# Linear attention and a top-1 mixture of experts on one core: loads in one queue, routing in small steps, scatters and fetches of separate rows told apart

## The chip, the cores and the metric

The kernel runs on 1 core of one Trainium2 chip. The metric is the device time of one execution in microseconds (us), as a median of several runs. The engines are TensorE (PE), VectorE (DVE), ScalarE (ACT), GpSimd (POOL) and SyncE (SP), which issues DMAs. Each has its own in-order list of instructions.

## The reference

Decayed linear attention over B = 4, H = 8, S = 768, D = 64, then every token goes through one of 8 experts.

```python
for b in range(nb):                       # blocks of the sequence
    intra = (qb @ kb.T * Dmask) @ vb
    out[:, :, sl] = intra + (qb * lam_pow) @ kv_state
    kv_state = lam_block * kv_state + (kb * rev_pow).T @ vb
x = out as (B*S = 3072 tokens) x (H*D = 512)
logits = x @ w_gate + modality_bias[modality_id]
e_idx = argmax(logits); gate_w = softmax(logits)[e_idx]
for e in range(8):                        # F = 1024
    out[mask] = gate_w[mask, None] * (relu(x[mask] @ w1[e]) @ w2[e])
```

With the seed's inputs four experts get tokens: 1,494, 1,319, 253 and 6.

## The kernel before

**Attention.** The kernel takes the sequence in chunks of 128: 24 blocks `g`, loaded in 12 pairs `m` by `load(m)`, 2 MB each, into `SLOTS` = 4 rotating buffers with the tag "load". Pairs 0 to 2 come in halves, pair 3 whole, on SP's queue; later pairs on ACT's. For a block, `scores` (PE, tile s), `mask` (DVE, pt), `keys` (ACT, kd), `query` (POOL, qd), `products` (PE, kv), `add` (DVE, state), `from_state` and `values` (PE, tile o; ACT copies to xt). After two pairs `turns` transposes their output on PE (`turn`, and line 303 and 305 copies to grp) and does the gate products (`gates`, tile x).

**Routing.** Tokens are routed in three batches of eight row tiles. `choose` finds each token's expert (one-hot `oh`), `ranks` counts on PE the tokens ahead of each in its expert, `slots_of` makes row numbers. `one_slot` then scatters one row tile, 128 rows of 528 floats, from grp to `placed` in DRAM by an indirect DMA on POOL; `jobs` is the list of scatters to do, `go`, `need` and `tick` take from it. `count` (PE) sums the tokens of each expert so far. After batch 0 `early_list` finds two tiles that are full (list A: tiles 0 and 1), after batch 1 two more (list B: tiles 2 and 3), after batch 2 `late_list` the rest (list C): tiles 4 and 5 of 64 and 32 rows (the thins), eight wide tiles 6 to 13, and up to nine more behind a branch. `put` puts a routing operation of DVE in a queue and `do(n)` gives out the next n of it.

**Experts.** A wide tile is 256 rows. `fetch_x` fetches its rows (xg, and idx for token and gate), `fetch_w1` and `fetch_w2` the expert's weights (raw1, raw2; the DMAs of a tile whose expert is that of the one before are skipped by a condition). `turn_rows` transposes the rows on DVE, `split_rows` and `split_w1` make two halves of each operand (ACT rounds, DVE subtracts). `first_layer` does four quarters on PE, `second` each 128 rows with three products per operand pair, then ACT scales by the gate (y) and POOL stores by token. Tile 0's first layer is done whole, without halves. `thin_first` and `thin_second` do the thins, their weights for tile 5 in `both1` and `both2`. `clear_ends` writes empty rows behind the last row of each expert, 8 DMAs of 256 rows with a register load each.

**What sets the order.** PE, DVE, ACT and SP execute in the order in which the code is written (`manual_schedule`); POOL's order is held by `pool`. DMAs wait for data by dependencies that the framework finds; two groups tell it that their rows differ (`apart`). In `placed`, every scatter and every fetch is otherwise a reader or writer of the same tensor, so a fetch stands behind all scatters written before it.

## Time and profile before

| | us |
|---|---|
| median of 3 runs (436.13 to 437.58) | 436.2 |
| the profiled execution | 436.5 |
| its span | 434.8 |
| TensorE busy | 398.2 |
| VectorE busy | 267.1 |
| ScalarE busy | 210.5 |
| GpSimd busy | 98.7 |

The span is from the first to the last recorded event; 1.7 us of the execution lie around it. Busy time counts an engine's own work and not its waits; matmuls overlap their weight loads. A stage's row gives the busy time of every engine inside it, and `PEclk` the share of the full TensorE clock that was granted. Stages of before, in us from the span's start: start to 33.5, pairs 2 to 11 to 115.9, tile 0 to 142.7, tile 1 to 172.3, tile 2 to 194.9, tile 3 to 219.8, thins to 244.8, wide tiles 6 to 13 to 424.6, end at 434.8.

### The profile page before, as it was taken

Reading aid. Unit: us, or ns where it says so; the run is one execution under the profiler, and the core shown is the slowest. Engines: PE = TensorE matmul, PEld = TensorE weight load, DVE = VectorE, ACT = ScalarE, POOL = GpSimd, SP = SyncE. Lnnn points to the kernel's source line nnn. Section 1 sums busy time; section 2 is a strip of 40 time slices with the busy share of each in tenths; the row PEclk is TensorE's granted clock in tenths of the full one; section 3 lists DMA queues with packets and bytes.
Section 4 is the critical chain, followed back from the end, with each engine's and each line's share of the span. In section 5 each row is a group of like instructions: output and inputs, shape, how many; then the busy total and the mean of one; then the engine's idle time right before and its main releaser. Section 6 shows DMA issues by size and latency. Waiting matters only on the chain.

```text
span 434.8 us, 9729 instructions
## 1 busy us (share of the span) xinstructions
PE 398.2 (92%) x3597; PEld 347.6 (80%) x3597; DVE 267.1 (61%) x494; ACT 210.5 (48%) x411; POOL 98.7 (23%) x125
## 2 busy tenths in 40 slices
PE   6879989699799979998968999999999999999990
PEld 4779879588588968978833798989898989898980
DVE  5638759777477656888320676667666666767510
ACT  1529568485445426418220646464646465555510
POOL 2815215550440238302000102020202020101000
PEclk8989999899899969999995999999999999999996
DMA  7998776947358973457359008787302020200100
GB/s 257 388 404 298 272 272 261 389 172 277 122 172 275 338 283 150 124 200 260 76 171 295 11 11 261 214 248 224 98 14 74 26 73 26 73 26 3 48 27 20
DMA packets 38216, 75.38 MB, mean 173 GB/s; under 512 B 6926, under 2 KB 19726, under 8 KB 37904
## 3 DMA queue, kind: packets, MB, share of 16 engines
q1 hardware_dynamic: 29728, 40.92, 29.7%
q10 hardware_dynamic: 4512, 20.97, 12.8%
q0 software_dynamic: 3920, 12.78, 7.7%
q8 instruction: 30, 0.49, 0.5%
q14 instruction: 26, 0.21, 0.2%
HBM read 90.57 MB, written 17.84 MB: 249 GB/s over the span
## 4 chain that ended last, share of the span: by engine, by line
issue 48%; PE 19%; DVE 11%; DMA 8%; POOL 6%; ACT 4%; POOLq 1%; ACTq 0%; SPq 0%; DVEq 0%
POOL out_dram L713 6%; DMA load<-in_qkv_dram 5%; DMA raw<-in_w_dram 3%; PE o L281 3%; PE o L299 2%; PE s L239 2%; PE s L689 2%; ACT kd L229 2%; PE o L273 2%; PE kv L689 2%; DVE pt L243 2%; DVE state L261 1%; DVE grp L303 1%; ACT xt L285 1%; DVE w2l L581 1%
## 5 line engine op out<-in xcount | busy, mean ns | idle before, releaser
L581 DVE TENSOR_TENSOR w2l<-raw,w2h 128x1024 fp32r<-128x1024 f32 x48 | 58.7, 1223 | 35.5 <-ACT w2h L580 34.8
L713 POOL DMA_INDIRECT out_dram<-y,idx x24 | 31.0, 1290 | 214.1 <-ACT y L712 191.1
L669 PE MATMUL o<-w2h,hh 128*128 128x512 f32 x192 | 75.2, 391 | 0.0
L670 PE MATMUL o<-w2l,hh 128*128 128x512 f32 x192 | 75.1, 391 | 0.0
L671 PE MATMUL o<-w2h,hl 128*128 128x512 f32 x192 | 74.9, 390 | 0.0
L581 DVE TENSOR_TENSOR w1l<-raw,w1h 128x1024 fp32r<-128x1024 f32 x44 | 51.3, 1222 | 3.6 <-ACT w1h L580 3.5
L669 PE MATMUL kv<-xh,w1h 128*128 128x256 f32 x176 | 51.1, 290 | 0.0
L669 PE MATMUL s<-xh,w1h 128*128 128x256 f32 x176 | 49.9, 284 | 1.1 <-ACT w1h L580 1.1
L670 PE MATMUL kv<-xl,w1h 128*128 128x256 f32 x176 | 50.7, 288 | 0.0
L671 PE MATMUL kv<-xh,w1l 128*128 128x256 f32 x176 | 50.5, 287 | 0.0
L671 PE MATMUL s<-xh,w1l 128*128 128x256 f32 x176 | 49.7, 282 | 0.8 <-DVE w1l L581 0.8
L580 ACT CAST w2h<-raw 128x1024 fp32r<-128x1024 f32 x48 | 49.8, 1038 | 0.0
L670 PE MATMUL s<-xl,w1h 128*128 128x256 f32 x176 | 49.7, 282 | 0.0
L580 ACT CAST w1h<-raw 128x1024 fp32r<-128x1024 f32 x44 | 43.1, 1045 | 1.7 <-DMA raw<-in_w_dram 1.7
L671 PEld LDWEIGHTS o<-w2h,hl 128*128 128x128 f32 x192 | 36.2, 188 | 7.6
L669 PEld LDWEIGHTS o<-w2h,hh 128*128 128x128 f32 x192 | 36.2, 189 | 7.3
L670 PEld LDWEIGHTS o<-w2l,hh 128*128 128x128 f32 x192 | 36.2, 188 | 7.2
L669 PEld LDWEIGHTS kv<-xh,w1h 128*128 128x128 f32 x176 | 34.1, 194 | 4.0 <-issue 3.8
L712 ACT ACTIVATE y<-o,idx 128x512 f32<-128x512 f32 x24 | 16.3, 683 | 42.1 <-PE o L671 42.1
L229 ACT ACTIVATE kd<-load,dk 128x64 f32<-128x64 f32 x144 | 35.6, 336 | 0.8 <-ACT grp L305 0.6
L216 POOL TENSOR_TENSOR qd<-load,pq 128x512 f32<-128x512 f32 x20 | 25.5, 1275 | 42.2 <-PE o L273 22.4
L669 PEld LDWEIGHTS s<-xh,w1h 128*128 128x128 f32 x176 | 33.0, 187 | 2.1 <-ACT w1h L580 1.6
(220 smaller groups left out, 674.2 us busy)
## 6 DMA issues: line engine op xcount, KB each, us to landing
raw<-in_w_dram SPq DMA_DIRECT2D x96, 512.0 KB
load<-in_qkv_dram ACTq DMA_DIRECT2D x8, 2048.0 KB
xg<-placed SPq DMA_DIRECT2D x48, 128.0 KB
placed<-blank SPq DMA_DIRECT2D x9, 528.0 KB
load<-in_qkv_dram SPq DMA_DIRECT2D x8, 512.0 KB
raw<-in_w_dram ACTq DMA_DIRECT2D x2, 2048.0 KB
both<-in_w_dram SPq DMA_DIRECT2D x8, 512.0 KB
load<-in_qkv_dram SPq DMA_DIRECT2D x2, 1024.0 KB
```

What stands on the lines that cost most here:

```text
L216: pool(nc.gpsimd.tensor_tensor(out=qds[g], in0=loaded(g)[1], in1=pq, op=ALU.mult))
L229: nc.scalar.activation(out=kds[g][:, p, hl, :], in_=kn[:, p, hl, :], func=AF.Copy, scale=dk[:, hl, p, P - 1 : P])
L239: nc.tensor.matmul(scs[g][:, hl, p, :], kt[r, p, :], qt[r, p, :], start=True, stop=True)
L281: nc.tensor.matmul(op[place(g, hl), p, :], vt[:, (2 * p + hl) * D : (2 * p + hl + 1) * D], pt[:, hl, p, :], start=(c == 0 and p == 0), sto ...
L580: nc.scalar.copy(out=hi, in_=src)
L581: nc.vector.tensor_tensor(out=lo, in0=src, in1=hi.bitcast(F32), op=ALU.subtract)
L669: nc.tensor.matmul(out, ah, bh, start=first, stop=False)
L670: nc.tensor.matmul(out, ah, bl, start=False, stop=False)
L671: return nc.tensor.matmul(out, al, bh, start=False, stop=last)
L689: mm = nc.tensor.matmul(hp[:, j, :], raw1[:, i, kc, fs], xt2[:, kc, :], start=(kc == 0), stop=(kc == KC - 1))
L712: nc.scalar.activation(out=y, in_=yp, func=AF.Copy, scale=idx[:, t, 1:2].bitcast(F32))
L713: sc = nc.gpsimd.indirect_dma_start(out=out, out_offset=bass.IndirectOffsetOnAxis(ap=idx[:, t, 0:1], axis=0), in_=y, in_offset=None, bound ...
```

## The change

1. All loads of q, k, v and of tile 0's weights go to SP's queue, the latter in four pieces of 512 KB and not one of 2,048 KB. `lamh` goes to ACT's.
2. The start is written out in another order; five more dummy matmuls; the identity is made first on POOL; a block's `query` waits for its first score product.
3. The routing's DVE work is given out in steps (`do(7)` per pair, `do(5)` after turns, `do(4)` in tiles), with fewer operations (`running` is a scan in place of a product and a sum). Ranks, counts and lists stand at other pairs, and so do the scatters (`aside`).
4. Scatters of batch b and fetches for lists A and B get groups of their own, so that a fetch waits for the scatters of its own batch and earlier ones alone. `xg` has two buffers. `fetch_x(0)` is at pair 8, `fetch_x(1)` at pair 9, `turn_rows(0)` at pair 10.
5. The last `turns` and its gates move inside tile 0's first layer; `ranks` of batch 2 come behind that layer, `count` behind the first quarter of tile 1.
6. Each clear becomes two, 64 rows always and 192 rows under a condition, each with a register load. `both1` is fetched ahead of `raw2` of tile 4, `both2` right behind it, into buffers of their own.
7. The last store of the fixed tiles goes to its own buffer and is issued behind the branches.
8. The scratch for POOL's DMA descriptors (`dynamic_dma_scratch_size`) is set to 2048; before, it is not given.

The core of the diff, with pieces left out that only rename, and the pieces that shorten the lists:

```diff
-                (nc.sync if m < SLOTS else nc.scalar).dma_start(out=halves[m], in_=source(m))
+                nc.sync.dma_start(out=halves[m], in_=source(m))
...
+                op = pool(nc.gpsimd.tensor_tensor(out=qds[g], in0=loaded(g)[1], in1=pq, op=ALU.mult))
+                if g in begun:
+                    after(op, begun.pop(g))
...
-            apart("slots", sc)
+            b = c // RC
+            for group in [f"slots{i}" for i in range(b + 1)] + [f"list{i}" for i in range(b)]:
+                tc.declare_no_dep(sc.ins, group=group, reason="rows differ")
+            tc.add_to_no_dep_group(f"slots{b}", sc.ins)
             return pool(sc, free=True)
...
-        def clear_ends():
-
-            for e in range(E):
-                vr = nc.sync.value_load(ends_at[0:1, e : e + 1], min_val=0, max_val=E * CAP - TT)
-                apart("ends", clear(bass.ds(vr, TT)))
+            if n < EARLY:
+                for f in fetches:
+                    for b in range(n // SOON + 1, RN):
+                        tc.declare_no_dep(f.ins, group=f"slots{b}", reason="rows differ")
+                    tc.add_to_no_dep_group(f"list{n // SOON}", f.ins)
+
...
+        def clear(at, rows, **kw):
+
+            p = rows // max(1, (rows + P - 1) // P)
+            return nc.sync.dma_start(out=placed[at, :].rearrange("(r p) w -> p r w", p=p),
+                                     in_=blank[:p].unsqueeze(1).to_broadcast([p, rows // p, RW]), **kw)
+
+        def clear_end(e):
+            vr = nc.sync.value_load(ends_at[0:1, 0, e : e + 1], min_val=0, max_val=E * CAP - TT)
+            for i in range(2):
+                if i == 0:
+                    c = clear(bass.ds(vr, XT), XT)
+                else:
+                    cr = nc.sync.value_load(ends_at[0:1, 1, e : e + 1], min_val=0, max_val=1)
+                    c = clear(bass.ds(vr + XT, TT - XT), TT - XT, cond=cr)
+                apart("ends", c)
+                for b in range(RN):
+                    tc.declare_no_dep(c.ins, group=f"slots{b}", reason="rows differ")
+                for b in range(2):
+                    tc.declare_no_dep(c.ins, group=f"list{b}", reason="rows differ")
...
                     tick(mm)
-            y = work.tile([P, DM], F32, name="y", tag="qd", bufs=4)
+            if hold:
+                y = const.tile([P, DM], F32, name="held")
+            else:
+                y = work.tile([P, DM], F32, name="y", tag="qd", bufs=4)
             nc.scalar.activation(out=y, in_=yp, func=AF.Copy, scale=idx[:, t, 1:2].bitcast(F32))
-            sc = nc.gpsimd.indirect_dma_start(
-                out=out, out_offset=bass.IndirectOffsetOnAxis(ap=idx[:, t, 0:1], axis=0),
-                in_=y, in_offset=None, bounds_check=N - 1, oob_is_err=False)
-            apart("tokens", sc)
-            pool(sc, free=True)
+
+            def store():
+                sc = nc.gpsimd.indirect_dma_start(
+                    out=out, out_offset=bass.IndirectOffsetOnAxis(ap=idx[:, t, 0:1], axis=0),
+                    in_=y, in_offset=None, bounds_check=N - 1, oob_is_err=False)
+                apart("tokens", sc)
+                pool(sc, free=True)
+
+            if hold:
+                behind.append(store)
+            else:
+                store()
         def thin_first(x, w):
```

```diff
         keys(0, True)
         scores(0)
         mask(0)
+        keep_busy(5)
         powers()
         from_state((0,))
         values(0)
+        block(1, True)
         products(0)
-        scores(1)
-        query(1)
-        keys(1, True)
         add(0)
-        mask(1)
+        scores(2)
+        mask(2)
+        query(2)
         from_state((1,))
         values(1)
         products(1)
-        for m in range(pairs):
+        keys(2)
+        add(1)
+        block(3)
+        gpsimd_constants()
+        load(SLOTS)
+        products(2)
+        products(3)
+        add(2)
+        add(3)
+        from_state((2, 3))
+        values(2)
+        values(3)
+        turns(0)
+        block(4)
+        block(5)
+        load(1 + SLOTS)
+        products(4)
+        products(5)
+        add(4)
+        for m in range(2, pairs):
             a, b = HB * m, HB * m + 1
             ahead = m + 1 < pairs
             add(b)
             if m == 4:
                 routed = 0, *choose(0, gate_rows())
-            elif m == 6:
+            elif m == 8:
+                routed = 1, *choose(1, gate_rows())
+            if ahead:
+                block(a + 2)
+                block(b + 2)
+            if m == 2:
+                routing_constants()
+            elif m == 3:
+                clear(slice(E * CAP, E * CAP + TT), TT)
+            elif m == 5 or m == 9:
+                ranks(routed[-1])
                 slots += slots_of(*routed)
                 jobs += [("slots", one_slot)] * RC
-            elif m == 7:
+            elif m == 6:
+                count()
                 early = early_list("A", listA)
-            elif m == 8:
-                routed = 1, *choose(1, gate_rows())
             elif m == 10:
-                slots += slots_of(*routed)
-                jobs += [("slots", one_slot)] * RC
-            if m == 0:
-                keys(2)
-                keys(3)
-            if ahead:
-                for i, g in enumerate((a + 2, b + 2)):
-                    scores(g)
-                    mask(g)
-                    if m > 0:
-                        keys(g)
-                    query(g)
-            do()
+                count()
+                early = early_list("B", listB, early)
+            do(7)
             go(aside.get(m, (0, 0))[0])
-            if m == 0:
-                gpsimd_constants()
-            else:
-                if m == 2:
-                    routing_constants()
-                from_state((a, b))
-                for g in (a, b):
-                    values(g)
-            if m == 3:
-                clear(slice(E * CAP, E * CAP + TT))
-            elif m == 5 or m == 9:
...
                 add(a + 2)
             go(aside.get(m, (0, 0))[1])
-            if m % 2:
+            if m % 2 and ahead:
                 turns(m // 2)
-            if m == 6:
-                count()
-            elif m == 8:
+                do(5)
+            if m == 8:
                 raw1 = w1_part("raw1", F32)
-                fetch_w1(*fetch_regs(0, True, nc.scalar), eng=nc.scalar)
+                fetch_w1(*fetch_regs(0, True))
+                fetch_x(0)
             elif m == 9:
                 raw2 = w2_part("raw2", F32)
-                fetch_w2(*fetch_regs(0, True, nc.scalar), eng=nc.scalar)
```

```diff
         def amid0(i):
-            nonlocal routed, slots, early
+            nonlocal routed, slots
+            if i < 2:
+                for tb in (2 * i, 2 * i + 1):
+                    turn(GR - 1, tb)
+                if i == 0:
+                    gates(GR - 1)
+                do(6)
+            elif i == 2:
+                do()
+                routed = 2, *choose(2, gate_rows())
+                do(4)
+            else:
+                do()
+
+        def amid1(i):
             if i == 0:
-                count()
-                early = early_list("B", listB, early)
-                do(10)
-            else:
-                do(8)
-
-        def amid1(i):
-            nonlocal routed, slots
-            if i == 0:
-                routed = 2, *choose(2, gate_rows())
-            elif i == 1:
-                do()
-            elif i == 2:
-                ranks(routed[-1])
-                slots += slots_of(*routed)
                 do()
                 jobs.extend([("slots", one_slot)] * RC)
                 count()
+                late_list(*early)
+            else:
+                do(4)
         def amid2(i):
-            if i == 0:
-                late_list(*early)
-            if i < 3:
-                do(12)
-            else:
-                do()
+            do(4)
         first_layer(amid0, whole=True)
+        need("slots")
         fetch_w1(*fetch_regs(1))
         fetch_w2(*fetch_regs(1))
+        fetch_x(2)
+        ranks(routed[-1])
         turn_rows(1)
         split_rows()
-        split_w1()
+        slots += slots_of(*routed)
+        split_w1(1)
+        fetch_w1(*fetch_regs(2))
         for t in range(2):
             second(0, t)
-        do()
-        fetch_x(2)
-        fetch_w1(*fetch_regs(2))
         first_layer(amid1)
         fetch_w2(*fetch_regs(2))
+        fetch_x(3)
         turn_rows(2)
         split_rows()
-        split_w1()
+        split_w1(4)
+        fetch_w1(*fetch_regs(3))
         for t in range(2):
             second(1, t)
```

```diff
         first_layer(amid2)
         fetch_w2(*fetch_regs(3))
         turn_rows(3)
         split_rows()
-        split_w1()
-        clear_ends()
-        for n in range(thins, wides + 1):
-            fetch_x(n)
+        split_w1(4)
+        for e in range(E):
+            clear_end(e)
         fetch_w1(*fetch_regs(thins))
         for t in range(2):
             second(2, t)
-
+        do()
+
+        both1 = w1_part("both1", F32, True)
+        both2 = [work.tile([P, 2, 2, DM], F32, name="both2", tag="xt", bufs=2) for i in range(2)]
+        both2 = [both2[i // 2][:, i % 2] for i in range(4)]
         first_layer()
+        for n in range(thins, wides + 1):
+            fetch_x(n)
+        fetch_w1(*fetch_regs(thins + 1, True), to=both1)
         fetch_w2(*fetch_regs(thins))
-        both1 = w1_part("both1", F32, True)
-        fetch_w1(*fetch_regs(thins + 1, True), to=both1)
+        fetch_w2(*fetch_regs(thins + 1, True), to=both2)
...
                 if n + 2 < fixed_ones:
                     fetch_w1(*fetch_regs(n + 2))
...
+        for store in behind:
+            store()
...
-    nc = _bacc.Bacc("TRN2", target_bir_lowering=False, num_devices=1)
+    nc = _bacc.Bacc("TRN2", target_bir_lowering=False, num_devices=1, dynamic_dma_scratch_size=2048)
```

Three places show how instructions move. In the rows, s and kv are the first layer's products, x the small tile of the routing, o the second layer's, hh and hl the two halves of the hidden layer, raw the weights as fetched.

PE, the end of tile 0's first layer. Before, with the count for list B behind its first quarter:

```order
L689 MATMUL s<-xt_127,raw_1387 128x256 x8
L422 LDWEIGHTS onesb
L422 MATMUL x<-ohsum,onesb 128x8
L689 MATMUL kv<-xt_127,raw_1387 128x256 x8
L689 MATMUL s<-xt_127,raw_1387 128x256 x8
L689 MATMUL kv<-xt_127,raw_1387 128x256 x8
L669 MATMUL o<-w2h,hh_1807 128x512
```

and after, with the last turn and the ranks of batch 2:

```order
L713 MATMUL s<-xt_127,raw_1390 128x256 x8
L312 MATMUL o<-ident,xt 128x128 x8
L323 MATMUL x<-xt,wgq 32x128 x16
L713 MATMUL kv<-xt_127,raw_1390 128x256 x8
L312 MATMUL o<-ident,xt 128x128 x8
L713 MATMUL s<-xt_127,raw_1390 128x256 x8
L713 MATMUL kv<-xt_127,raw_1390 128x256 x8
L375 LDWEIGHTS lowb
L375 MATMUL x<-oh,lowb 128x64
L376 LDWEIGHTS onesb
L376 MATMUL x<-ohsum,onesb 128x64
```

The count left the layer; between its last products and the second layer stand now the ranks, which read `oh`.

DVE, tile 1's first layer and the routing of batch 2. Before:

```order
L581 TENSOR_TENSOR w2l<-raw_1556,w2h 128x1024
L697 SCALAR_TENSOR_TENSOR hl_1810<-s,hh_1808 128x512
L335 TENSOR_TENSOR pos<-oh,x 128x64
L335 TENSOR_REDUCE slot<-pos 128x8
L335 TENSOR_SCALAR m8s<-m_2093 128x8
L335 TENSOR_REDUCE ohn<-oh 128x8
L335 TENSOR_TENSOR ohsum<-ohsum,ohn 128x8
L335 TENSOR_REDUCE sm<-l 128x8
```

and after:

```order
L597 TENSOR_TENSOR w1l<-raw_1390,w1h 128x1024
L348 TENSOR_REDUCE ohn<-oh 128x8
L597 TENSOR_TENSOR w2l<-raw_1590,w2h 128x1024
L721 SCALAR_TENSOR_TENSOR hl_1795<-s,hh_1793 128x512
L348 TENSOR_TENSOR ohsum<-ohsum,ohn 128x8
L348 TENSOR_REDUCE sm<-l 128x8
```

`ohsum`, which the count on PE reads, stands behind the third quarter's `hl` before, and behind the first quarter's after.

SP, the clears of tile 2's time. Before, two of the eight:

```order
L615 TENSOR_LOAD ends_at
L615 ISA x2
L609 ISA
L609 DMA placed<-blank 256x1x528
L615 TENSOR_LOAD ends_at
L615 ISA x2
L609 ISA
L609 DMA placed<-blank 256x1x528
```

and after, one expert's:

```order
L637 TENSOR_LOAD ends_at
L637 ISA x2
L633 ISA
L633 DMA placed<-blank 64x528
L642 TENSOR_LOAD ends_at
L642 ISA x2
L633 ISA
L633 DMA placed<-blank 96x2x528
```

Behind them, before, the last issues ahead of tile 5's first weights:

```order
L652 DMA raw_1556<-in_w_dram 128x1024
L652 ISA
L652 DMA raw_1556<-in_w_dram 128x1024
L652 ISA
L652 DMA raw_1556<-in_w_dram 128x1024
L632 TENSOR_LOAD listC
L632 ISA x2
L644 ISA
L644 DMA both_2969<-in_w_dram 128x1024
```

and after, the last of those weights and what follows:

```order
L672 DMA both_2854<-in_w_dram 128x1024
L672 ISA
L672 DMA both_2854<-in_w_dram 128x1024
L664 TENSOR_LOAD listC
L664 ISA x2
L667 TENSOR_LOAD listC
L667 ISA x2
L676 ISA
L676 DMA raw_1590<-in_w_dram 128x1024
```

One clear became two loads and two DMAs, and `raw` of the second layer no longer stands ahead of `both`.

## Rows read from the trace of the kernel before

**Rows 1.** The page, part 1: TensorE's busy time, its share of the span, instructions.

```profile
PE 398.2 (92%) x3597; PEld 347.6 (80%) x3597; DVE 267.1 (61%) x494; ACT 210.5 (48%) x411; POOL 98.7 (23%) x125
```

**Rows 2.** Stages: length, busy us (x instructions) by engine, PE's clock, DMA share, GB/s.

```profile
0.00:33.47 33.47, 26.59 (x347) 21.25 (x347) 17.36 (x43) 10.91 (x34) 13.74 (x37) 0.90 0.95 351
33.47:115.93 82.46, 74.39 (x1379) 65.52 (x1379) 62.23 (x152) 54.79 (x187) 30.76 (x36) 0.98 0.71 261
115.93:142.72 26.79, 26.79 (x115) 22.64 (x116) 18.37 (x43) 11.51 (x15) 7.83 (x13) 0.94 0.65 225
142.72:172.27 29.55, 25.88 (x156) 23.63 (x156) 17.61 (x33) 12.50 (x17) 12.99 (x15) 0.88 0.74 250
...
194.90:219.76 24.86, 22.96 (x146) 20.57 (x148) 15.26 (x20) 11.82 (x16) 4.04 (x3) 1.00 0.48 159
219.76:244.84 25.08, 19.14 (x167) 9.63 (x167) 3.71 (x6) 5.43 (x9) 1.97 (x2) 0.73 0.64 203
244.84:424.63 179.79, 179.79 (x1156) 164.17 (x1152) 114.36 (x123) 95.03 (x124) 21.61 (x16) 1.00 0.29 88
```

**Rows 3.** The same view for stretches in which the granted clock was half.

```profile
25.30:28.60 3.30, 3.30 (x43) 2.97 (x39) 0.77 (x1) 0.28 (x1) 0.00 (x0) 0.50 1.03 408
83.30:86.60 3.30, 3.30 (x26) 2.97 (x27) 1.97 (x4) 2.23 (x8) 0.15 (x1) 0.50 1.03 422
117.40:120.70 3.30, 3.30 (x9) 2.64 (x8) 0.32 (x1) 0.00 (x0) 2.75 (x5) 0.50 0.44 169
...
226.60:240.20 13.60, 11.48 (x54) 4.71 (x56) 0.69 (x1) 0.38 (x1) 0.00 (x0) 0.50 0.87 282
```

**Rows 4.** Timeline of PE: start, us, operation, times; in brackets idle before, releaser.

```profile
23.64 0.60 PE L239 MATMUL s<-load 64*128 64x128 f32 x6 [2.86 <-DMA load<-in_qkv_dram]
...
82.53 1.70 PE L299 MATMUL o<-ident,xt 128*128 128x128 f32 x8 [3.57 <-ACT grp L305]
...
115.93 4.98 PE L689 MATMUL s<-xt,raw 128*128 128x256 f32 x14 [1.99 <-DVE xt L657]
...
155.41 0.17 PE L422 MATMUL x<-ohsum,onesb 128*128 128x8 bf16 x1 [3.66 <-DVE ohsum L335]
...
231.09 3.19 PE L729 MATMUL s<-both,xf 128*32 128x256 f32 x25 [0.70 <-DMA both<-in_w_dram]
```

**Rows 5.** Timeline of SP's queue (issues), tiles 2 and 3.

```profile
188.01 11.66 SPq L609 DMA_DIRECT2D placed<-blank  x8
202.43 1.93 SPq L598 DMA_DIRECT2D xq<-placed  x4
...
216.81 1.36 SPq L644 DMA_DIRECT2D raw<-in_w_dram  x4
...
222.09 1.98 SPq L644 DMA_DIRECT2D both<-in_w_dram  x4
```

**Rows 6.** Batch 0's scatters: landing (line 394), two issues, SP's fetch behind them.

```profile
DMA to landing us min/median/max: 4.5/7.2/9.1
...
73.91 0.98 POOL L394 DMA_INDIRECT placed<-grp,sloti  x1 [0.28 <-ACT kd L229]
...
75.39 1.07 POOL L394 DMA_INDIRECT placed<-grp,sloti  x1 [0.28 <-POOL grp L393]
...
100.81 2.49 SPq L598 DMA_DIRECT2D xg<-placed  x4
```

**Rows 7.** Timeline of ACT and DVE: a quarter's end, two routing operations.

```profile
131.85 0.60 ACT L696 ACTIVATE hh<-kv 128x512 fp32r<-128x512 f32 x1 [1.92 <-PE kv L689]
132.48 0.69 DVE L697 SCALAR_TENSOR_TENSOR hl<-kv,hh 128x512 fp32r<-128x512 f32 x1 [0.66 <-ACT hh L696]
...
151.09 0.22 DVE L335 TENSOR_TENSOR oh<-eq,m 128x64 bf16<-128x64 f32 x1
...
155.19 0.17 DVE L335 TENSOR_TENSOR ohsum<-ohsum,ohn 128x8 bf16<-128x8 bf16 x1
```

**Rows 8.** Timeline of POOL: the last store.

```profile
425.63 0.99 POOL L713 DMA_INDIRECT out_dram<-y,idx  x1 [4.45 <-ACT y L712]
```

187 lines of the change are left out of this document (96 added, 91 removed).

## The prediction

> **What bounds the kernel now.** I read the header of the page first: TensorE (PE) is busy for 398.2 us of the span [rows 1]. So time can come only from PE's idle time (36.6 us), from stretches in which its clock was granted at half, and from the two ends. The table by stage says where [rows 2]. The eight wide tiles at the end are PE from end to end at a granted clock of 1.00: 179.79 us, 22.47 us each. That is the price of a tile, and every early tile above it has slack: tile 1 takes 29.55, tile 3 24.86. The pairs m = 2 to 11 hold 82.46 - 74.39 = 8.07 us of PE idle, the start 6.88, the thin section 5.94. A second table gives the clock [rows 3]: stretches of 3.3 us at 0.50 (1.2 of 2.4 GHz) lie at 25.3, 83.3 and 117.4, and 13.6 us around the thins. Each follows a wait of PE. A half-clock stretch of 3.3 us costs up to 1.65 us.
>
> The waits themselves are in PE's timeline [rows 4]: 2.86 us for a load in the start; 3.57 before the turn of pair 7, where VectorE (DVE) was busy with list A; 1.99 before tile 0, for the transpose of its tokens; 3.66 before the count in tile 1, for `ohsum`; and the last of the waits for `both1` in the thins. Then I read SP's queue over tiles 2 and 3 [rows 5], which decides when `both1` comes, the scatters [rows 6], two short DVE and ACT chains [rows 7], and the tail [rows 8].
>
> **The change, part by part.** All against the profiled execution, 436.5 us (span 434.8 and 1.7 around it); that is 0.3 over the median of 436.2.
>
> *Start.* Blocks 2 to 5 are put in another order, so that the state and value products of blocks 2 and 3 and turn 0 stand ahead of the scores that waited 2.86 us for their load [rows 4]. More work than the wait is moved ahead of it, so the wait goes, and the half clock behind it (1.65) with it [rows 3]: **-4.5**. Bounds: -2, if the loads, already 351 GB/s in this stage [rows 2], come no sooner and a part of the wait comes back at pair 3; -6, if the extra five dummy products also save some of the 1 to 2 us waits around block 0.
>
> *Pairs.* The routing of a batch is done in small steps between the pairs' own DVE work, with fewer operations. The 3.57 us went on DVE doing list A in one go; it goes. The 1.99 us before tile 0 go, since the tokens are fetched during pair 8 and turned during pair 10. Of the remaining 2.5 us I leave 1.0. That is -7.1, and -1.65 for the half clock at 83.3: **-8.7**. What hides the moved work: DVE is busy 62.23 of the 82.46 us [rows 2], so it has some 20 us to spare; if the steps fall in front of a block's mask, the cover is gone and waits of that size stay (bound -4). Turn 5 and its gate products move into tile 0: PE's work, the same on either side, nothing.
>
> The cover of the early fetch is thinner. In before the fetch for tile 0 was issued at 100.81, when the last scatter of batch 0 had landed [rows 6]. After, all eight are issued by pair 8, by my count at about 79; with the longest landing of 9.1 us [rows 6] that is 88, and with some 5 us for the fetch and 1.3 for the turn about 95, before tile 0's start at about 99. Three to four us to spare. SP's queue waits in that fetch meanwhile, and the four pieces of `raw2` stand behind it; they are wanted only some us after tile 0's start.
>
> *Tile 0.* Its half clock at 117.4 followed the 1.99 us wait: -1.65. New: PE does the ranks of batch 2 right behind the first layer and must wait there for the one-hot `oh`, which DVE makes after the last quarter's `hl`. From the rows: about 0.2, the ACT pass `hh` 0.60, `hl` 0.69, two steps of 0.22 [rows 7], about 1.9. Bounds: 0, if DVE does the two steps ahead of `hl`; 3.66, the wait that the same thing cost in tile 1 of before [rows 4]. I take +1.9, the chain as the order has it. Together **+0.25**.
>
> *Tile 1.* It falls to a plain tile's 22.47 from 29.55, -7.1 [rows 2]: the 3.66 us wait goes with the half clock behind it, and the weights are asked for earlier. The count still stands on PE, after the first quarter, behind `hh` 0.60, `hl` 0.69 and `ohsum` 0.17 [rows 7] with about 0.2 of passing on: +1.65. **-5.4**.
>
> *Tiles 2, 3 and the thins* go by SP's queue, not by PE. In before the clears start at 188.01 and `both1` is first issued at 222.09 [rows 5], 34.1 us later: eight clears with their register loads 11.7, loads of the lists 2.8, three fetches 14.4 (with the two loads ahead of `raw`), `raw1` skipped 1.4, then `raw2` skipped and three more loads, 3.9. After, each clear is two DMAs and two register loads. A skipped issue is 0.34 (four in 1.36), a register load 0.6 to 0.85 (the 3.9 us less four skipped issues, by three, with or without their set-up): a skipped clear 0.95 to 1.2, and I take 1.0. A clear that is done takes 1.46, one of 64 rows somewhat less, 1.25. By the seed's counts two of the eight second clears are done: 8 x 1.25 + 6 x 1.0 + 2 x 1.46 = 18.9, of which 0.8 is the first load, ahead of the first issue. Then `raw1` with its loads 2.9, the three fetches 13.6, `both1` 1.05, `raw2` now behind it: 35.7, which is +1.6 (bounds -2 and +6, for clears of 15 and 23.4). On the other side the chain starts sooner: DVE does 4 list operations per quarter in tile 2 and not 12, which I put at -2.3 (8 x 0.2 to 0.3, the size of `oh` [rows 7]). So from tile 2's start to tile 6's start, 72.6 us in before [rows 2]: **-0.7** (bounds -5 and +4). Tile 3's own 2.4 us over a plain tile [rows 2] are gained by PE and given back in the wait for `both1`, since tile 3 then ends 44.9 us after tile 2's start and `both1` is issued at about 49.
>
> *Wide tiles:* 0. *Tail.* PE ends at 424.63 [rows 2], 10.2 us before the end of the span. In before the last store is issued until 426.62 [rows 8], and 8.2 us follow: its landing, and the branches over the conditional tiles and the close. After, the branches come first. Nothing shows how the 8.2 divide; bounds 0 and -5. The landing no longer stands ahead of the branches, so I take **-3.0**. *New clock loss:* one stretch of half clock behind the two new waits, **+1.7**.
>
> The sum: -4.5 - 8.7 + 0.25 - 5.4 - 0.7 - 3.0 + 1.7 = -20.35, so 416.1 for the profiled execution and about **415.8** for a median.
>
> **The rivals.**
>
> *Main case (0.62):* the sum, 410 to 420 with its nearer bounds.
>
> *R1, the small ring, the slower end (0.04).* The program's scratch for the descriptors that POOL writes is set to 2,048 bytes. If that room holds one scatter only, a scatter waits until the one before has landed, 7.2 us in the middle of batch 0 [rows 6]; eight make 58 us from about 66, so the last lands at 124 and not at 88. Tile 0 then starts at about 130, 28 us late: 415.8 + 28 = 444. The point from which it decides is one scatter in flight: with two, eight take 29 us, to 95, and tile 0 is late by 3 us. Against it: in before two scatters are issued 1.5 us apart and none lands in under 4.5 [rows 6], so two at least were in flight; nothing shows how much room they took. The Trainium skill, "SBUF — State Buffer", section "SBUF size: 192, 224, or 256?", calls a scratch of 16 KiB per partition the ring that POOL's descriptors live in, and "DMA: Bandwidth & Descriptors", section "Terms", gives a descriptor 16 B. By these 2,048 bytes are an estimated 128 descriptors, room for a scatter of 128 rows even on one ring, and R1 would not bite; no run here shows it.
>
> *R2, the thins no longer wait for `both1` (0.10).* If the clears come cheaper and start sooner by some 10 us together, tile 6 starts when tile 3 and the thins' PE work are through: 44.9 + 19.14 x 0.73 = 58.9 us after tile 2's start and not 71.9. That is 13 us less, 403. Against it: the issues counted above.
>
> *R3, the waits only move (0.20).* DVE's routing is spread over more places; if PE waits a little at each, the pairs keep their 8 us in small pieces, and both new waits halve the clock: 415.8 + 7.1, less some 2 because the pieces are smaller, + 1.65, some 422.5. For it: three of the waits in the pairs end on DVE or on ACT behind it.
>
> **How the numbers follow.** About 0.5% (2.2 us) is what a measurement here can tell from no change. Main, R2 and R3 are faster, 0.92, and with what is left between them 0.94; R1 is slower, 0.04; some mishap that eats all within 0.5%, 0.02. The likeliest is the sum, 415.8. The range goes to R2's side, 403.5, and takes in R3's to 424.
>
> **What would show it.** Right: no PE wait for a load at the end of the start and none at the turn of pair 7; tile 0 starting at about 99 without a wait for `xt`; one wait of 1.5 to 2 us before tile 0's second layer and one after tile 1's first quarter, each for DVE; tile 1 at some 24 us; clears of 16 to 20 us on SP in tile 2 and a wait of several us for `both1`; 7 us behind PE's end. Wrong: scatters issued only one landing apart (R1); tile 6 starting 60 us after tile 2 (R2); many PE waits of under 1 us on DVE in the pairs (R3). The sum fails most easily at SP's queue, where one term of 23 us is counted by issues, and at the tail.

## The result, and the profile after

| | us | of before |
|---|---|---|
| before, median of 4 runs | 436.89 (436.13 to 438.76) | |
| changed, median of 4 runs | 426.04 (424.69 to 426.70) | 0.9742, 95% interval 0.9697 to 0.9786 |
| changed, profiled execution | 424.69, span 423.0 | before 436.5, span 434.8 |

The change made the kernel 10.8 us faster. The forecast was 415.8, range 403.5 to 424.0: the sign was right, half of the gain is missing, and the time lies 2 us outside the range. The profiled execution gained 11.8 where the sum had 20.35.

First the header line of TensorE on the page, the counterpart of [rows 1], then the table by stage, cut at the same instructions as [rows 2] (length, busy us with instructions of PE, PEld, DVE, ACT and POOL, granted clock, DMA share, GB/s). Tile 2, tile 3 and the thin section are the fifth to seventh line.

```profile
PE 393.4 (93%) x3602; PEld 343.9 (81%) x3602; DVE 261.9 (62%) x478; ACT 211.1 (50%) x411; POOL 96.8 (23%) x126
```

```profile
0.00:32.11 32.11, 27.66 (x350) 20.45 (x350) 17.18 (x40) 12.47 (x40) 13.38 (x37) 1.00 0.91 344
32.11:112.55 80.44, 72.53 (x1334) 64.36 (x1332) 59.31 (x159) 49.49 (x171) 38.01 (x47) 0.96 0.88 303
112.55:144.32 31.77, 29.85 (x172) 25.16 (x170) 19.75 (x39) 15.78 (x26) 1.00 (x1) 0.95 0.62 170
144.32:168.52 24.20, 22.66 (x146) 20.57 (x145) 17.42 (x45) 12.35 (x16) 15.83 (x18) 1.00 0.88 292
168.52:190.96 22.44, 22.44 (x145) 20.52 (x144) 17.83 (x44) 12.35 (x16) 2.11 (x3) 1.00 0.17 50
190.96:213.50 22.54, 22.54 (x146) 20.34 (x144) 10.84 (x22) 7.51 (x10) 2.25 (x2) 1.00 0.36 105
213.50:237.00 23.50, 16.08 (x168) 8.52 (x167) 5.36 (x9) 5.57 (x9) 1.96 (x2) 0.85 0.82 239
237.00:416.62 179.62, 179.62 (x1154) 163.98 (x1152) 114.25 (x123) 94.92 (x124) 21.28 (x16) 1.00 0.30 88
416.62:422.98 6.36, 0.00 (x0) 0.00 (x0) 0.00 (x0) 0.69 (x1) 0.98 (x1) 0.69 0.10 34
```

The same view for the stretches at half clock (1.2 of 2.4 GHz), which answer [rows 3]:

```profile
105.00:111.80 6.80, 4.08 (x48) 3.78 (x50) 3.31 (x13) 0.00 (x0) 5.29 (x9) 0.50 0.82 286
132.30:135.70 3.40, 3.40 (x9) 2.67 (x8) 2.49 (x4) 2.85 (x4) 0.00 (x0) 0.50 0.79 237
221.00:227.80 6.80, 4.58 (x22) 1.28 (x26) 1.29 (x2) 1.23 (x3) 0.00 (x0) 0.50 0.98 357
```

Against the sum's terms, with turn 5 (110.59 to 113.95 in before, 3.36 us) counted to tile 0 on both sides:

| stage | before | after | change | forecast |
|---|---|---|---|---|
| start | 33.47 | 32.11 | -1.36 | -4.5 |
| pairs 2 to 11, without turn 5 | 79.10 | 80.44 | **+1.34** | **-8.7** |
| tile 0, with turn 5 | 30.15 | 31.77 | +1.62 | +0.25 |
| tile 1 | 29.55 | 24.20 | -5.35 | -5.4 |
| tile 2 to tile 6 | 72.57 | 68.48 | -4.09 | -0.7 |
| wide tiles | 179.79 | 179.62 | -0.17 | 0 |
| tail | 10.17 | 6.36 | -3.81 | -3.0 |
| new half clock, in the stages above | | | | +1.7 |

Ten of the missing microseconds are in the pairs, and over half of them at pair 11. PE's timeline there (start, us, operation, times; in brackets the idle time before and its releaser):

```profile
101.60 0.63 PE L264 MATMUL kv<-load,kd 128*64 128x64 f32 x16
102.16 0.44 PE L286 MATMUL o<-qd,state 64*64 64x128 f32 x4
107.72 1.97 PE L286 MATMUL o<-qd,state 64*64 64x128 f32 x28 [5.12 <-issue]
```

PE stands still for 5.12 us, the longest wait ahead of the thin section, and the half clock of 105 to 111.8 sets in during it. It waits for the state of the next block, DVE's sum `state<-state,pq,kv`. DVE's timeline:

```profile
103.60 0.21 DVE L348 TENSOR_TENSOR deltaB<-deltaB,ntB 128x8 f32<-128x8 f32 x1
107.30 0.85 DVE L274 SCALAR_TENSOR_TENSOR state<-state,pq,kv 128x64 f32<-128x64 f32 x4 [3.49 <-remote]
```

DVE was done with its routing at 103.81 and then waited 3.49 us itself, for `kv`, whose products PE had ended by 102.23. Nobody works in that gap on whose result the sum depends. What runs meanwhile is POOL with batch 1's scatters, one every 1.47 us, and, issued on SP behind the four pieces of tile 0's `raw2`, the fetch of tile 1's tokens:

```profile
102.14 0.98 POOL L407 DMA_INDIRECT placed<-grp,sloti  x1 [0.28 <-issue]
...
103.61 0.98 POOL L407 DMA_INDIRECT placed<-grp,sloti  x1 [0.28 <-issue]
```

```profile
95.25 4.09 SPq L676 DMA_DIRECT2D raw<-in_w_dram  x4
100.13 1.87 SPq L615 DMA_DIRECT2D xg<-placed  x4
```

An engine tells another that a piece of its work is done by updating a semaphore, a counter that the other waits for. The trace also records when these updates take effect. The nine updates of PE for the last `pt` product and the eight `kv` products that ended between 101.76 and 102.23 are recorded at

```
102.79 103.53 104.27 105.02 105.75 105.80 106.50 106.55 107.27
```

six of the steps 0.70 to 0.75 us wide, two to a scatter's 1.47, and DVE starts 0.03 us behind the last. So by the trace the products were done and the news of it came late. Counted over the whole trace (instructions of PE, DVE, ACT and POOL whose update is recorded 0.25 us or more after their end, or not at all), there are 91 such in this trace. All but five lie in 67 to 78, 84 to 87, 100 to 112 and 150 to 166 us, wherever scatters run, and the five at 170 and 193 stand behind POOL's indirect stores; the trace of before has none. Such a count is rough: some updates may be missing from the record and not late, and it depends a little on how updates are matched to instructions. PE's ends are modelled, but 56 of the 91 are of the other engines.

### The profile page after: what moved, and what is told of

The parts are those of the page before. It is cut to its first block, busy times and chain, and to the rows that moved or that the text cites. A ratio compares the mean times of both kernels' runs of the same rounds, so it can differ in the third digit from the quotient of the medians.

```text
span 423.0 us, 9783 instructions
## 1 busy us (share of the span) xinstructions
PE 393.4 (93%) x3602; PEld 343.9 (81%) x3602; DVE 261.9 (62%) x478; ACT 211.1 (50%) x411; POOL 96.8 (23%) x126
## 4 chain that ended last, share of the span: by engine, by line
issue 48%; PE 35%; POOL 6%; DVE 5%; DMA 3%; ACT 2%; POOLq 1%; DVEq 0%; ACTq 0%
POOL out_dram L744 5%; PE o L294 5%; PE s L251 5%; PE kv L264 3%; PE o L286 3%; PE o L695 3%; PE o L693 3%; PE o L694 3%; PE o L312 3%; PE s L713 2%; DMA lamh<-in_lam_dram 1%; DVE grp L316 1%; DMA out_dram<-y,idx 1%; PE kv L693 1%; ACT kd L233 1%
## 5 line engine op out<-in xcount | busy, mean ns | idle before, releaser
L744 POOL DMA_INDIRECT out_dram<-y,idx x23 | 29.1, 1263 | 228.0 <-ACT y L741 228.0
L693 PE MATMUL kv<-xh,w1h 128*128 128x256 f32 x176 | 49.5, 281 | 0.0
```

The source lines that it names most:

```text
L693: nc.tensor.matmul(out, ah, bh, start=first, stop=False)
L744: sc = nc.gpsimd.indirect_dma_start(out=out, out_offset=bass.IndirectOffsetOnAxis(ap=idx[:, t, 0:1], axis=0), in_=y, in_offset=None, bound ...
```

## The experiments

Each result carries the number of the chip that it ran on, and each ratio is to the kernel before on the same chip. Chips 9 and 12 come first, 1 and 13 later. In the texts on record, A and A2 put the cause at the scratch's size. "Ring" is short for that scratch, in which POOL's DMA descriptors lie.

**1. Is it the small ring?** Four sizes of scratch. In before:

```diff
-    nc = _bacc.Bacc("TRN2", target_bir_lowering=False, num_devices=1)
+    nc = _bacc.Bacc("TRN2", target_bir_lowering=False, num_devices=1, dynamic_dma_scratch_size=2048)
```

> The kernel before with one edit: the scratch for POOL's DMA descriptors is 2,048 bytes. Theory A (the small scratch makes the other engines' semaphore updates late while scatters run, which cost the changed kernel some 11 us in its pairs): updates of PE, DVE and ACT that come 0.25 us or more after the instruction's end, of which the kernel before has none, appear around its scatters at 72 to 92 and 106 to 126; the time rises by 3 to 12 us over before, to 440 to 449. Theory B (the late updates come from loads, row fetches and scatters sharing the DMA engines, whatever the scratch): no late updates, 436 to 437.5, same as before.

In the changed kernel 8192, and likewise 4096:

```diff
-    nc = ... num_devices=1, dynamic_dma_scratch_size=2048)
+    nc = ... num_devices=1, dynamic_dma_scratch_size=8192)
```

> The changed kernel with a scratch of 8,192 bytes and nothing else. Theory A: the late updates go, the 5.1 us wait of PE in pair 11 and its half clock go, the pairs with scatters lose their extra 3 and 1 us: 413 to 418. If even 8,192 is too small, something between 418 and 426. Theory B: 425 to 427, the same waits in the same places.

> The changed kernel with a scratch of 4,096 bytes. Theory A with a room that is used up by a few scatters: between the kernels of 2,048 and 8,192 bytes, 415 to 424, fewer late updates than with 2,048. Theory A with a mere threshold: as 8,192. Theory B: 425 to 427.

And the size that before has (not given), with room made for it:

```diff
-                y = const.tile([P, DM], F32, name="held")
+                y = work.tile([P, DM], F32, name="held", tag="xt", bufs=2)
...
-    nc = ... num_devices=1, dynamic_dma_scratch_size=2048)
+    nc = ... num_devices=1)
```

> The changed kernel without the small scratch (the default, as in the kernel before); so that it fits, the held result of the last store goes into a buffer that is free by then. Theory A2 (late semaphore updates come with any scratch below the default): none of them, no 5.1 us wait in pair 11, 413 to 419. Theory B (scatters beside loads and row fetches on the DMA engines): 425 to 428 and the same waits.

The kernel before, unedited, on that same chip, for its updates:

> The kernel before once more, for a trace beside the others of this call. Theory A2: no late semaphore updates, as in its first trace. Theory B, in which one trace without them was chance: a dozen or two, as with the small scratch. Time 434 to 439 under both.

| kernel | chip | us | ratio, 95% interval | late updates |
|---|---|---|---|---|
| before, ring 2048 | 9 | 436.16 | 0.9975 (0.9931 to 1.0019) | 32 |
| changed, ring 8192 | 9 | 428.24 | 0.9772 (0.9715 to 0.9830) | 88 |
| changed, ring 4096 | 9 | 425.95 | 0.9735 (0.9663 to 0.9807) | 87 |
| changed, ring not given | 12 | 425.29 | 0.9681 (0.9602 to 0.9761) | 73 |
| before | 12 | 436.74 | | 21 |

No size of the ring takes the late updates away, and no time of the changed kernel is clear of the others by its interval. The wait in pair 11 is 5.19 with a ring of 4096, and it stays with one of 8192 and with the full one:

```profile
109.14 1.13 PE L286 MATMUL o<-qd,state 64*64 64x128 f32 x16 [5.14 <-issue]
```

```profile
107.61 1.09 PE L286 MATMUL o<-qd,state 64*64 64x128 f32 x28 [3.61 <-issue]
```

A and A2 fall. The kernel before has late updates on these chips too, 21 and 32 of them, but loses nothing that can be seen by them. B, which is left, had expected none in the kernel before with the small ring, and it says nothing of chips.

**2. Scatters, or the fetch beside them?** Once without scatters in pairs 10 and 11 (they then go out behind tile 0's first-layer products), once with the fetch of tile 1's tokens later:

```diff
-        aside = {6: (0, 3), 7: (1, 2), 8: (1, 1), 10: (2, 2), 11: (2, 2)}
+        aside = {6: (0, 3), 7: (1, 2), 8: (1, 1)}
```

> The changed kernel with batch 1's eight scatters taken out of pairs 10 and 11; they are issued one by one behind products of tile 0's first layer. Theories A2 and B: no scatters, no late updates at 101 to 112; the 5.1 us wait and its half clock (some 7 us together) go from pair 11, and some of it may come back in tile 0 or as a late fetch for tile 2: 418 to 424. Theory C (the wait in pair 11 has nothing to do with the scatters, but with the fetches alone): 425 to 428, the wait stays.

```diff
                 fetch_w2(*fetch_regs(0, True))
-                fetch_x(1)
...
         fetch_w1(*fetch_regs(1))
+        fetch_x(1)
         fetch_w2(*fetch_regs(1))
```

> The changed kernel with the row fetch of tile 1 moved from pair 9 to behind tile 1's first weights, so that its packets of 512 bytes don't run beside batch 1's scatters. Theory B and theory C: the 5.1 us wait shrinks to under 2 us, 418 to 423, unless tile 1's rows now come late. Theory A2: the wait stays, 425 to 428.

Both on chip 12, with the small ring, where the kernel with the full ring took 425.29 (423.67 to 426.67). Without the scatters: 418.28 (417.04 to 420.59), ratio 0.9519 (0.9444 to 0.9595), 7.0 less. With the fetch later: 422.63 (421.56 to 425.09), ratio 0.9643 (0.9559 to 0.9728), some 2.7 less, with ranges that overlap. PE in pair 11 without the scatters, then with the fetch later:

```profile
105.36 0.89 PE L286 MATMUL o<-qd,state 64*64 64x128 f32 x24 [1.50 <-DVE state L274]
```

```profile
102.54 0.46 PE L264 MATMUL kv<-load,kd 128*64 128x64 f32 x9 [0.47 <-issue]
...
105.46 1.16 PE L286 MATMUL o<-qd,state 64*64 64x128 f32 x28 [2.10 <-issue]
```

Without scatters the wait is 1.50, has its plain cause (DVE does a run of list B's steps ahead of the sum), and the pairs have no half clock. With the scatters but less to load beside them, 2.57 remain. So on this chip it is the scatters that cost the time. That loads beside them make it worse is a hint and not shown: in the five profiles with scatters and fetch in place, on chip 9, on chip 12 and on that of the first runs, the wait is 2.83 to 5.19, and 2.57 lies only just below.

**3. The start: `lamh`.** In the changed kernel the load of `lamh` (4 KB, 32 bytes to each of 128 partitions) is issued on ACT's queue, at the same time as the first block's load on SP's. Put back on SP's, ahead of that load, in the changed kernel and in the one without the scatters:

```diff
-        nc.scalar.dma_start(out=lamh, in_=lam.rearrange("h o -> (h o)").partition_broadcast(P))
+        nc.sync.dma_start(out=lamh, in_=lam.rearrange("h o -> (h o)").partition_broadcast(P))
```

> The changed kernel with only the load of lamh put back on SP's queue. Theory L: first scores at 5.6 to 5.9 us, 1 to 2 us off the changed kernel's 426.0: 424 to 425, the wait in pair 11 as before. Rival: no difference, 425.5 to 426.5.

> The kernel of e6 (no scatters in pairs 10 and 11) with one more part undone: the load of lamh goes back to the head of SP's queue. Theory L: beside the first loads on the DMA engines, its 128 packets of 32 bytes delay them and themselves; at the head of the queue the first scores start at 5.6 to 5.9 us and not at 7.0 to 7.8, and the time is 1 to 2.5 us under e6's 418.3: 416 to 417.5. Rival: the start is set by something else behind the first scores, and the time stays within 0.7 us of e6.

On chip 9: 420.70 (419.88 to 422.20), ratio 0.9636 (0.9605 to 0.9667), against 425.95 and 428.24 in the first group; and 416.32 (414.23 to 416.95), ratio 0.9535 (0.9508 to 0.9563). Queue ACT of the changed kernel at its start, then SP's, then PE's first products:

```profile
0.84 0.42 ACTq L75 DMA_DIRECT2D lamh<-in_lam_dram  x1
```

```profile
0.83 3.78 SPq L93 DMA_DIRECT2D load<-in_qkv_dram  x6
```

```profile
6.96 1.16 PE L251 MATMUL s<-load 64*128 64x128 f32 x16 [1.66 <-DMA load<-in_qkv_dram]
8.06 1.25 PE L823 MATMUL o<-busy 128*128 128x512 bf16 x5
```

and with `lamh` on SP's, SP and PE:

```profile
0.83 0.41 SPq L75 DMA_DIRECT2D lamh<-in_lam_dram  x1
1.29 2.74 SPq L93 DMA_DIRECT2D load<-in_qkv_dram  x5
```

```profile
5.56 1.16 PE L251 MATMUL s<-load 64*128 64x128 f32 x16 [0.48 <-DMA load<-in_qkv_dram]
```

The load is issued 0.46 us later and its data are there 1.40 us sooner. The Trainium skill, "DMA: Bandwidth & Descriptors", section "Issuing engines are not separate DMA queues", says that DMAs of several engines run on the same 16 DMA engines and that a second issuer saves only the issuing; the trace agrees, the saving being 0.46 us. The start became 30.65 us long, 1.46 less than in the first profile. This is no chance of one run: in all seven profiles with `lamh` on ACT's queue the first scores start at 6.57 to 7.87 and the start is 31.75 to 35.01 us long; in all six with it on SP's they start at 5.54 to 5.76, and it is 30.65 to 30.81. How so small a load delays the large one no run shows. The rest of the 5.3 us is not the start's: pair 11's wait is 2.83 in that run, and tile 0 has no half clock. The text on record had expected that wait as before, and 424 to 425; why it shrank is open. The two kernels of this group, run together on one chip, differ by the scatters alone: 4.4 us.

**4. `both1` ahead of the row fetches.** The wait for `both1` is 5.5 us in the changed kernel. Fetched ahead of the three row fetches, in the second kernel of group 3:

```diff
         first_layer()
+        fetch_w1(*fetch_regs(thins + 1, True), to=both1)
         for n in range(thins, wides + 1):
             fetch_x(n)
-        fetch_w1(*fetch_regs(thins + 1, True), to=both1)
```

> The kernel of e8 with the fetch of both1 ahead of the three row fetches in SP's queue. If SP's queue alone sets when the thins get their weights, both1 is issued some 13 us sooner, PE's wait of 5 us for it goes and the row fetches, 3 us later, still come in time: 3 to 6 us under e8, 411 to 414. Rival: the row fetch of tile 4 now comes late and the wait only changes its name: within 1 us of e8.

416.65 (415.88 to 418.23), ratio 0.9546 (0.9516 to 0.9576), on chip 9 beside 416.32: no difference. PE:

```profile
207.36 3.67 PE L765 MATMUL s<-raw,xf 128*64 128x256 f32 x32 [1.58 <-DVE xf L681]
...
219.15 1.12 PE L776 MATMUL x<-ident,hn 128*128 128x128 f32 x4 [6.25 <-ACT hn L769]
```

and ACT:

```profile
217.46 1.14 ACT L596 CAST xh<-xt 128x512 fp32r<-128x512 f32 x2 [7.65 <-DVE xt L681]
218.51 0.86 ACT L769 ACTIVATE hn<-s 128x512 f32<-128x512 f32 x2
```

The wait changed its name. The fetches that now come later are those of the thins' own tokens (1.58) and of tile 6's, and ACT splits tile 6's tokens ahead of `hn`. The rival on record was right; by my reading SP's queue sets the sum of both.

**5. The two new waits.** Where the changed kernel waits for `oh` and `ohsum`, the ranks were put behind tile 0's first half of the second layer and the count behind tile 1's second quarter (edit against the second kernel of group 3), and once more without the five dummy products:

```diff
-        ranks(routed[-1])
...
-        slots += slots_of(*routed)
-        split_w1(1)
+        split_w1()
         fetch_w1(*fetch_regs(2))
-        for t in range(2):
-            second(0, t)
+        second(0, 0)
+        ranks(routed[-1])
+        slots += slots_of(*routed)
+        do()
+        second(0, 1)
...
                 jobs.extend([("slots", one_slot)] * RC)
+            elif i == 1:
                 count()
                 late_list(*early)
+                do(4)
```

> The kernel of e8 with the two new waits of PE on routing taken away by order alone: ranks of batch 2 behind the first half of tile 0's second layer, count behind the second quarter of tile 1. If these waits cost what they show (1.92 and 1.54 us) and nothing else is late: 3.0 to 3.8 us under e8's 416.3, 412.5 to 413.3; a half clock behind them, where a run has one, goes too. Rival: DVE's later slots make the weights' halves or the scatters of batch 2 late, within 1 us of e8.

```diff
-        keep_busy(5)
```

> The kernel of e11 without the five dummy products ahead of block 0's values. If they only lie on the path: 1.25 us less in the start, 411.3 to 412. If they keep PE's clock up, as the half clock at 8.2 us of the kernel before without them suggests: the start's half clock comes back, and the time is 0 to 2 us over e11.

On chip 1: 409.40 (408.20 to 409.82), ratio 0.9386 (0.9341 to 0.9432), and 410.19 (409.46 to 410.67), ratio 0.9408 (0.9363 to 0.9454). The dummies earn at most a little, 0.8 us, and none of that in the start: with and without them its granted clock is 1.00, and pair 3's scores, which end it, begin at the same time. In both kernels:

```profile
30.68 0.49 PE L251 MATMUL s<-load 64*128 64x128 f32 x4
```

Both new waits are gone, with one of another kind in tile 1 for them:

```profile
131.65 0.38 PE L695 MATMUL s<-xh,w1l 128*128 128x256 f32 x1 [1.06 <-DVE w1l L597]
```

**6. The same two kernels on one more chip.** After group 5 the time lay 3 us under what the text on record had expected, and the count of late updates had dropped from 57 (second kernel of group 3, chip 9) to 1 (both of group 5, chip 1), more than an edit in tiles 0 and 1 explains. So the changed kernel was run unedited beside the unedited first kernel of group 5:

> The changed kernel once more, unedited, on whichever chip. Theory D (late updates belong to the chip): if e14 beside it has none, this one has none either, its wait in pair 11 is under 2.5 us, and the time is 417 to 421; if e14 has them, it is 425 to 427 as before. Theory E (the order of e11 keeps them away): late updates and the 5.1 us wait here, 425 to 427, and none in e14.

> The kernel of e11 unedited on the same chip as e13. Theory D: late updates here if and only if e13 has them; with them 411 to 414, without them 408.5 to 410. Theory E: none, 408.5 to 410, whatever e13 shows.

On chip 13: 417.11 (415.57 to 418.83), ratio 0.9549 (0.9507 to 0.9592), and 410.76 (408.77 to 411.26), ratio 0.9391 (0.9352 to 0.9429). The changed kernel, with nothing edited, is 9 us faster here than on the chip of its first runs; late updates: 0 and 1. Its stages up to tile 1, then those of the other kernel of this group, both as above:

```profile
0.00:33.94 33.94, 29.07 (x350) 21.04 (x350) 17.18 (x40) 12.47 (x40) 13.44 (x37) 0.95 0.92 348
33.94:105.34 71.40, 68.65 (x1334) 61.58 (x1332) 58.67 (x159) 49.80 (x172) 33.98 (x41) 1.00 0.87 306
105.34:135.53 30.19, 28.27 (x172) 24.01 (x170) 19.75 (x39) 15.19 (x25) 5.95 (x8) 1.00 0.77 224
135.53:159.73 24.20, 22.66 (x147) 20.59 (x145) 17.46 (x45) 12.34 (x16) 15.81 (x18) 1.00 0.91 308
```

```profile
0.00:30.72 30.72, 27.94 (x350) 20.76 (x351) 17.17 (x40) 12.47 (x40) 13.37 (x37) 1.00 0.93 347
30.72:102.11 71.39, 68.65 (x1335) 61.57 (x1333) 58.66 (x159) 49.79 (x172) 28.63 (x32) 1.00 0.92 319
102.11:130.26 28.15, 28.15 (x171) 23.93 (x170) 14.80 (x32) 15.19 (x25) 12.93 (x16) 1.00 0.71 231
130.26:153.70 23.44, 22.70 (x147) 20.54 (x145) 22.03 (x53) 12.35 (x16) 16.85 (x17) 1.00 0.96 321
```

PE of the changed kernel in pair 11, and at its start:

```profile
99.87 0.64 PE L264 MATMUL kv<-load,kd 128*64 128x64 f32 x16
...
102.42 1.09 PE L286 MATMUL o<-qd,state 64*64 64x128 f32 x28 [1.56 <-DVE state L274]
```

```profile
7.87 1.61 PE L251 MATMUL s<-load 64*128 64x128 f32 x16 [2.65 <-DMA load<-in_qkv_dram]
```

The pairs take 71.40 and not 80.44, with POOL's scatters 1.47 us apart as before and the same fetch beside them. And the scatters' move is worth nothing on this chip: 71.39 without them in pairs 10 and 11. By this, what it earned in groups 2 and 3 came from the late updates. From one kernel to the other the profiled execution goes from 416.46 to 410.68: start -3.22 (`lamh`), pairs -0.01, tile 0 -2.04, tile 1 -0.76 (the two waits), tile 2 to tile 6 +0.25.

## Where the prediction failed, and where it held

*Pairs (-8.7; measured +1.34).* This is the step that failed. Its mechanism held: the waits for list A and for tile 0's tokens went, and where updates are in time the term is 71.40 - 79.10 = -7.70. What failed is the list of what can go wrong: "if the steps fall in front of a block's mask" was the one bound, and a wait of PE for work that was already done was in no row of before. It stood where scatters had been pulled into the pairs, on the chips where that makes updates late. The two sides differ by 9.04 us. Of these 5.48 lie from pair 11's scores to tile 0: the wait (5.12 against 1.56), and the half clock around it, which can cost 2.04, half of the 4.08 us for which PE was busy in it. Pair 7 has 2.86, in waits of under 0.4 and in products drawn out between them, and pair 8 has 0.70.

*Start (-4.5; measured -1.36, and +0.47 on chip 13).* The wait of 2.86 and the half clock behind it went as forecast, and so did one more half clock of before, from 8.2 to 11.5, that the sum had not counted; on chip 13 that one is there again. Against this gain stands what the sum had at nothing. `lamh` on another queue: first scores at 6.96 (7.87 on chip 13) against 5.85 before; with it on SP's queue 5.56, and a start of 30.65, -2.8. The five dummies, 1.25 us of PE's time, are no such term, since the start is as long without them (group 5). The `kv` products may be one: 3.37 us for blocks 2 and 3 in the changed kernel,

```profile
17.42 3.37 PE L264 MATMUL kv<-load,kd 128*64 128x64 f32 x32
```

where before took 2.46, while a group of 16 takes 0.63 when its keys are ready. I read this as PE keeping step with ACT, which makes these keys from 16.46 to 20.40; no run shows it apart. The bounds, -2 to -6, took the case that the loads "come no sooner" and left out that they come later.

*Tile 0 (+0.25; measured +1.62, and +0.04 on chip 13) and tile 1 (-5.4; measured -5.35 on both).* Both new waits came where the order has them, and of the forecast size, 1.9 and 1.65:

```profile
131.52 0.19 PE L375 MATMUL x<-oh,lowb 128*128 128x64 bf16 x1 [1.92 <-DVE oh L348]
...
148.90 0.17 PE L436 MATMUL x<-ohsum,onesb 128*128 128x8 bf16 x1 [1.54 <-DVE ohsum L348]
```

Tile 0's excess is the half clock of 132.3 to 135.7 behind the first. The term for that, +1.7, is right here; on chip 13 the same wait of 1.93 has no half clock behind it, and the one stretch there lies at 8.4 to 11.8, behind the wait for the first load.

*Tile 2 to tile 6 (-0.7; measured -4.09).* SP's queue was counted well. The clears and `both1` in its timeline, then PE's wait:

```profile
181.13 19.83 SPq L633 DMA_DIRECT2D placed<-blank  x16
...
218.01 1.96 SPq L672 DMA_DIRECT2D both<-in_w_dram  x4
```

```profile
222.69 2.22 PE L765 MATMUL s<-both,xf 128*32 128x256 f32 x4 [5.52 <-DMA both<-in_w_dram]
```

The clears start 12.6 us into tile 2 (before 15.7) and take 19.83 (forecast 18.1); `both1` is issued 49.5 us into it, forecast about 49, before 49.8 [rows 2, 5]. The miss lies behind that issue, where the sum had no term: from it to tile 6 before took 22.75 us and the changed kernel 18.99. `raw2`, which now stands behind `both1`, has no part in it: its four issues are skipped in both kernels and move nothing, at 0.34 us each with their set-up. Before, then after:

```profile
219.70 1.34 SPq L652 DMA_DIRECT2D raw<-in_w_dram  x4
...
221.50 1.36 SPq L676 DMA_DIRECT2D raw<-in_w_dram  x4
```

PE's clock is at half for 6.8 us there and not for 13.6 [rows 3], with PE busy for 4.58 and not 11.48 us of it. Half of the difference is 3.45, so the clock can make nearly all of the 3.76; no run tried it apart.

*Tail (-3.0; measured -3.81).* The last store is issued 1.3 us behind PE's end (before 1.0), and 4.1 us follow its issue where 8.2 did [rows 8]:

```profile
417.94 0.98 POOL L744 DMA_INDIRECT out_dram<-held,idx  x1 [4.77 <-ACT held L741]
```

So the term's estimate was short by 0.8. By my reading the branches had about half of the 8.2 us, and the landing with the close the rest; no run took them apart.

*The rivals.* R1 fell with the result's own trace: with 2,048 bytes POOL issues scatters 1.47 us apart, and before none landed in under 4.5 [rows 6]; group 1 agrees. The Trainium skill's figures ("SBUF — State Buffer", section "SBUF size: 192, 224, or 256?", and "DMA: Bandwidth & Descriptors", section "Terms"), by which 2,048 bytes are an estimated 128 descriptors, did not decide it: room for one scatter of 128 rows on one ring is the very condition under which R1 was to bite, and not, as the prediction has it, a reason against it. R1's price was also low by its own numbers: tile 0 at 130 and not 99 is 31 us late, not 28. R2 did not come: the wait for `both1` is 5.52. R3 gave 422.5, nearer to the time than the main case, by another mechanism: its many small waits on DVE aren't there; one large wait is, and not on DVE's work. And the 417.1 of chip 13 is near 415.8 partly by terms that cancel: start 5.0 too hopeful and pairs 1.0, against 2.9 in the thins, 0.8 in the tail and the 1.7 for the clock.

## What to carry to other kernels

Before an indirect scatter is pulled into a stretch in which engines hand each other small results, ask what a late hand-over would cost there: a trace without such hand-overs, from one chip, says nothing on it, and the same kernel should be timed on several chips before a few per cent are believed. A tiny load with a small piece for every partition was better ahead of the first large load in the same queue than beside it in another. And when a wait has several causes in one queue, moving one of them only renames it (group 4); the work that the waiting engine needs has to be moved (group 5, 409.4 us, the fastest version here).

## What the runs showed of the hardware

**Semaphore updates can come microseconds late, on some chips.** Each row is a profiled execution:

| kernel | chip | late or missing updates: PE, DVE, ACT, POOL together | us |
|---|---|---|---|
| changed, first runs | not recorded | 91 | 424.69 |
| changed, ring 8192; 4096 | 9 | 88; 87 | 429.33; 424.64 |
| changed, ring not given | 12 | 73 | 426.67 |
| changed, no scatters in pairs 10, 11 | 12 | 65 | 420.59 |
| the same, `lamh` on SP | 9 | 57 | 414.23 |
| changed | 13 | 0 | 416.46 |
| ranks later | 1; 13 | 1; 1 | 409.82; 410.68 |

It isn't the record alone that is late: DVE starts behind the last update, PE loses 5.12 us, and the kernel 9. The Trainium skill, "Perfetto Trace Analysis", section "Per-instruction lifecycle: what the profiler-reported window actually captures", says that on every engine the passing on of an update falls outside the instruction's slice; the trace agrees, the wait of 3.49 us showing only as idle time. It gives no length for it. Shown: the long wait in pair 11 needs scatters there (without them it is the plain 1.50), no size of the ring takes it away, and chips 9 and 12 had late updates in every profile of the changed kernel and its variants there, 1 and 13 in none to speak of. Open: whether loads beside the scatters matter; what differs between these chips, and whether it is the chip or the hour, since only chip 9 was used at two times; on which chip the first trace of before, without late updates, was taken; and whether the recording of a trace takes part, since every execution here has its span and clock from one. That scatters make the updates pass at two per 1.47 us would fit a path shared with POOL's descriptors; that is argued from the steps of 0.70 to 0.75 us and not shown.
